# Splitting the loads of double-precision weights, and the GpSimd addition that joins their halves, in an RWKV-7 and quick-GELU kernel

## Chip, cores and metric

One core of a Trainium2 chip runs the kernel. Times are device microseconds of one execution (µs). The time before is the median of three runs, 713.35 µs (712.49 to 715.39).

## What is computed

The reference joins a recurrent attention block and a two-layer block. The recurrence has a 40x40 state for each of 4 batches and 8 heads, over 768 steps; its output, 3072 tokens by 320 channels, goes through two weight matrices with a GELU between them:

```python
for t in range(S):
    y[:, :, t] = np.einsum('bhd,bhde->bhe', rt, state)
    Sa = np.einsum('bhde,bhe->bhd', state, at)
    state = state * wt[:, :, None, :] - np.einsum('bhd,bhe->bhde', Sa, bt) \
            + np.einsum('bhd,bhe->bhde', vt, kt)
x = y.transpose(0, 2, 1, 3).reshape(B * S, H * D)      # 3072 x 320
h = x @ w_in                                           # 320 x 2048
out = (h / (1 + np.exp(-1.702 * h))) @ w_out           # 2048 x 320
```

The activations are float32. The two weight matrices arrive as 8-byte floating-point numbers, because a float32 array times a double scalar is double.

## The kernel before

**Attention.** The sequence is cut into 12 chunks of 64 steps. A chunk and a pair of batches make a *unit*, so there are 24 units. A unit loads its inputs (`load`, L525, and `load_w`, L518), takes logarithms and exponentials of the decay (`decay`, L568), scales its inputs (`prep`, L643), inverts a triangular matrix in five levels (`inverse`, L692: matmuls into `ps_level`, a copy to SBUF at L780 or L813, a transpose at L752 or L731), and solves for its output and the new state (`solve`, L859). The output `x` is written to DRAM and read back transposed as `xT` (`part_with`, L979, and `get_back`, L985), because the two-layer block wants channels on partitions.

**The two-layer block.** For every pair of units, `mlp` (L995) runs the up-projection (`ps_up`), the GELU on ScalarE (L1008) and the down-projection (`ps_down`). All matmuls go through one helper, L330, so the profile tells them apart by the names of their PSUM tiles. The PE instruction stream holds one weight load for each matmul: 20,256 of each.

**The weights.** They stay in SBUF as float32, in `w_sb`. `weight(n, rank, src)` (L462) brings in one of eight *pieces*, each 128 partitions by 1280 numbers of 8 bytes (1280 KB), and turns it into float32 by work on its two 32-bit words. The steps of a piece are:

- L498, SyncE's queue (SP): one transfer from DRAM into a place named by `raws`: a region of `extra`, an unused region of `w_sb`, or two slots of `xT_all`.
- L478, ScalarE: `rebased`, the high word scaled to the float32 exponent.
- L482, L486 and L490, VectorE (DVE): `bounded`, `shifted` and `rounded`, each over 1280 elements.
- L494, GpSimd (POOL): `joined`, an int32 addition of the two parts over 1280 elements, after which the piece counts as `weight`.

Pieces 0 to 3 are `w_in` and 4 to 7 are `w_out`. The first five are loaded in the opening, the others when an earlier piece has left its place.

**What sets the order.** No order is written by hand. Each step is added to a `Plan` (L60) with a rank, the engines that may run it, a cost in ns, what it reads and writes, and for SP steps a size. `Plan.order` (L105) then simulates the engines: whenever an engine is free it takes the runnable step of lowest rank. Its model of the transfers is one wire, used in the order of issue, at 417 bytes per ns with a factor of 1.3, and 2010 ns of latency. It also models the fetch of PE instructions in blocks of 256 (L67): a fetch takes 3528 ns and is stretched while a transfer is under way, with weight 0.35, or 0.63 if the transfer is larger than 1e6 bytes (L68, L204). For POOL and for DVE work in SBUF the model serializes the two engines (L197). `refined` (L247) tries 300 random changes of ranks for steps that start in the first 140 µs and keeps those that shorten the modelled time. So each change of a cost or of a step's size can give another order on every engine in the opening. The emitted program keeps that order for each engine, and waits are put in wherever data or buffers need them.

The ranks of the pieces are `RANKS`, L299: 14, 16, 20, 24, 35, 37, 39, 41. Unit i's loads have rank 10i - 4, its scalings 10i - 6, its solve steps about 10i.

Of the kernel before, what the change touches and what calls it, by code (L numbers as in the profile page):

```python
# [19 lines left out]
INT32 = mybir.dt.int32  # L20
UINT32 = mybir.dt.uint32
INT64 = mybir.dt.int64
ALU = mybir.AluOpType
# [256 lines left out]
def rwkv7_gelu_quick(ctx: ExitStack, tc: tile.TileContext, time_d, v_d, w_d, wc_d, ak_d, b_d, rv_d, w_in, w_out, out):  # L280
    nc = tc.nc
# [5 lines left out]
    PIECE = w_in.shape[2]  # L287
# [6 lines left out]
    EARLY = 4  # L294
    BY_PE = 4
    PLAIN = 4
    ROUNDS, WINDOW, SHARE = 4, 5000.0, 1.0
    TRIES, SEED = 300, 1
    RANKS = [14, 16, 20, 24, 35, 37, 39, 41]  # L299
    HALF = [slice(0, 64), slice(64, 128)]  # L300
    BITS = (0, 1)
# [8 lines left out]
    plan = Plan(dict(logw=3, wc=3, G=1, wch=3, wz=2, time=2, ak=2, b=2, rv=2, FT=3, GT=1, kh=2, bh=2, zr=2, rz=2,  # L310
                     A=1, B=1, RV=2, E0=2, W0=2, P21=2, PT=2, W=2, E=2, ES=2, EX=2, T=2, Tc=1, QT=1, zraw=2, zT=1, M=2, x=1, xT=3, g=4, ob=1), 4)
# [17 lines left out]
    def mm(o, lhsT, rhs, start):  # L329
        nc.tensor.matmul(o, lhsT, rhs, start=start, stop=True, skip_group_check=True)  # L330
# [5 lines left out]
    def pe(*sets):  # L336

        return {"PE": sum(n * 2 * max(58.0, cols / 1.2 + 3) for n, cols in sets), "instr": sum(16 * n for n, _ in sets)}

    def dve(n):  # L340
        return {"DVE": 170.0 + 1.03 * n}

    def act(n):
        return {"ACT": 210.0 + 0.76 * n}
# [7 lines left out]
    def of(e):  # L352
        return nc.gpsimd if e == "POOL" else nc.vector
# [77 lines left out]
    def preset(engine, *places):  # L431
        for t in places:
            copy(engine)(t, one32.unsqueeze(1).to_broadcast([128, 8, 32]))
# [28 lines left out]
    def weight(n, rank, src):  # L462
        at = raws[n]
        def raw():
            if at == "x":
                return xT_all[:, 1:].rearrange("p s n -> p (s n)").bitcast(INT64)
            tile, k = spots[at]
            return tile[:, k * PIECE:(k + 2) * PIECE].bitcast(INT64)

        scale = lambda: w_sb[:, n * PIECE:(n + 1) * PIECE].bitcast(INT32)  # L470

        before = [("weight", m) for m in range(n) if raws[m] == at]
        there = [("weight", m) for m in range(n) if raws[m] in (f"w{n}", f"w{n - 1}")]
        word = lambda dt, w: raw().bitcast(dt).rearrange("p (n two) -> p n two", two=2)[:, :, w]

        def rebased(t):

            nc.scalar.activation(scale().bitcast(FP32), word(FP32, 1), ACT.Prelu, scale=2.0 ** -112, alpha=2.0 ** 32)  # L478

        def bounded(t):  # L480

            nc.vector.tensor_scalar(scale().bitcast(FP32), scale().bitcast(FP32), least, most, ALU.max, ALU.min)  # L482

        def shifted(t):

            nc.vector.tensor_single_scalar(scale(), scale(), 3, op=ALU.logical_shift_left)  # L486

        def rounded(t):

            nc.vector.tensor_single_scalar(word(INT32, 1), word(UINT32, 0), 2.0 ** -29, op=ALU.mult)  # L490

        def joined(t):

            nc.gpsimd.tensor_tensor(out=scale(), in0=scale(), in1=word(INT32, 1), op=ALU.add)  # L494

        one, add = 170.0 + 0.52 * PIECE, 200.0 + 2.1 * PIECE
        T = lambda *names: [(name, n) for name in names]
        plan.add(rank, {"SP": 350.0}, lambda t: nc.sync.dma_start(raw(), src), reads=before, writes=T("wt"), size=128 * PIECE * 8)  # L498
        plan.add(rank, act(PIECE), rebased, reads=T("wt") + there, writes=T("rebased"))
        plan.add(rank, {"DVE": one, "sbuf": True}, bounded, reads=T("rebased"), writes=T("bounded"))  # L500
        plan.add(rank, {"DVE": one, "sbuf": True}, shifted, reads=T("bounded"), writes=T("parts"))
        plan.add(rank, {"DVE": one, "sbuf": True}, rounded, reads=T("rebased"), writes=T("parts"))
        plan.add(rank, {"POOL": add}, joined, reads=T("parts"), writes=T("weight"))

    def weights():
        for n in range(len(raws)):
            weight(n, RANKS[n], w_in[n] if n < NQ else w_out[n - NQ])
# [184 lines left out]
    def inverse(i):  # L692
# [10 lines left out]
        PT = at(PT_t, i).rearrange("p (j t) -> p j t", t=96)  # L703
        if i < PLAIN:
            plan.add(R - 3, {"ACT": 400.0}, lambda t: preset(t.engine, PT[:, :, 64:]), room=T("PT"), writes=T("preset"))
        elif i < PLAIN + 2:
            plan.add(R - 3, {"ACT": 800.0, "DVE": 900.0}, lambda t: preset(t.engine, at(E0_t, i), at(W0_t, i)[:, :, 32:]), room=T("PT"),
                     writes=T("preset"))

        def score_N(t):  # L710

            ps = psum(t, "ps_N")
            for f, u in product(BITS, BITS):
                for e, b in QUARTERS:
                    o, j = (2 * f + u) * 64, slot(b, u, f)
                    mm(ps[HALF[b], e, o:o + 64], ahT()[HALF[e], j], b_of(i)[HALF[e], j], o == 0)
        plan.add(R, pe((4, 64)), score_N, reads=T("ahT", "bhT") + (T("preset") if i < PLAIN + 2 else []), uses=T("ak", "b"), room=T("E0", "P21"), pair=("N", i))
        for n in BITS if i >= PLAIN else ():
            plan.add(R, dve(256), lambda t, n=n: nc.vector.copy_predicated(  # L719
# [4 lines left out]
                 writes=T("P21"), pair=("N", i))  # L724
        if i >= PLAIN:
            plan.add(R, {"DVE": 430.0, "POOL": 750.0, "sbuf": True}, lambda t: of(t.engine).tensor_sub(  # L726
                at(W0_t, i)[:, :, :32], two32.unsqueeze(1).to_broadcast([128, 8, 32]), at(E0_t, i)), reads=T("E0"), writes=T("W0"))

        def turned(rank, source, reads, n, dst, writes):

            plan.add(rank, dve(256), lambda t: nc.vector.transpose(ES(n), source(t)), writes=[key("ES", n, 6)], **reads)  # L731

            def spread(t):
                if t.engine == "ACT":
                    for h in BITS:
                        nc.scalar.activation(dst[:, :, h], ES(n), ACT.Copy, scale=quads[:, h, :1])  # L736
                else:
                    of(t.engine).tensor_mul(dst, ES(n).unsqueeze(2).to_broadcast([128, 8, 2, 32]),
                                            quads.unsqueeze(1).to_broadcast([128, 8, 2, 32]))
            plan.add(rank, {"POOL": 1390.0, "DVE": 700.0, "ACT": 910.0, "sbuf": True}, spread, reads=[key("ES", n, 6)], writes=writes)  # L740

        if i >= PLAIN:
            turned(R, lambda t: at(E0_t, i), dict(reads=T("E0")), 0, EX(0), [key("EX", 0, 5)])
# [411 lines left out]
```

## Time and profile before

| What | Value |
|---|---|
| Median of three runs | 713.35 µs |
| Profiled execution, its own time | 715.64 µs |
| Span of its instructions | 713.9 µs |
| PE busy over the span | 673.0 µs, 94% |
| DVE, ACT and POOL busy | 423.8, 347.7 and 204.6 µs |
| Pieces (L498), transfers | 8, of 1280 KB |
| Issue of such a transfer on SP | 0.33 to 0.41 µs |
| Addition L494, eight times | 2.94 to 3.48 µs |
| L482, L486 and L490, median | 0.82 µs each |
| L478, median | 1.39 µs |

The profile is of one execution, by engine: PE is matmul, PEld is PE's weight load, DVE is VectorE, ACT is ScalarE, POOL is GpSimd, and SPq is the queue of SyncE, which here issues all transfers. A line of a timeline gives the start, the duration, the engine, the line of the code and the instruction with its tiles; a count after x says that a row merges several instructions. In the chain of waits, "issue" is time in which an engine waited for nothing that the records show. The windows give, for a stretch of time, each engine's busy µs and number of instructions, then the clock granted to PE (1.00 is full), the share in which the DMA engines were busy, and GB/s.

### The profile page before, as it was taken

The page shows a single profiled execution, that of the slowest core. Times are in us where ns is not written, and L with a number is a line of the kernel's source. Part 1 is how long each engine was busy: PE and PEld are TensorE (multiplying, and loading weights), DVE is VectorE, ACT ScalarE, POOL GpSimd, SP SyncE. Part 2 cuts the span into 40 slices and gives each one's busy share as a digit, 9 for nine tenths or more (in the row PEclk, how much of TensorE's full clock was granted, in tenths as well). Part 3 has the DMA queues.
Part 4 walks back from the last instruction along what each step waited for, and adds up shares of the span by engine and source line. Part 5 has one row for each costly group of instructions (what it writes and reads, how often), then busy time and mean ns, then how long its engine had stood idle before and what let it go on. Part 6 is the DMA issues. An engine that isn't in the chain of part 4 may idle for free.

```text
span 713.9 us, 43522 instructions
## 1 busy us (share of the span) xinstructions
PE 673.0 (94%) x20256; PEld 562.4 (79%) x20256; DVE 423.8 (59%) x747; ACT 347.7 (49%) x683; POOL 204.6 (29%) x260
## 2 busy tenths in 40 slices
PE   4667899999999999999999999999999999999997
PEld 4566779887888788788888998779978788877563
DVE  6689777756766576577474775666675656421000
ACT  4465636656365465454555565256445535342020
POOL 5367244442431321331342233220341320200000
PEclk9879999999999999999999999999999999999999
DMA  7955351431441341341432241251341230111000
GB/s 244 394 193 181 111 168 47 139 99 44 129 121 32 113 137 32 111 139 42 120 121 86 72 124 50 83 147 33 107 115 32 81 96 5 41 49 31 20 3 19
DMA packets 31860, 69.81 MB, mean 98 GB/s; under 512 B 5056, under 2 KB 14272, under 8 KB 30656
## 3 DMA queue, kind: packets, MB, share of 16 engines
q1 hardware_dynamic: 31680, 67.03, 30.5%
q8 instruction: 159, 2.61, 1.5%
q14 instruction: 21, 0.17, 0.1%
HBM read 59.15 MB, written 7.86 MB: 94 GB/s over the span
## 4 chain that ended last, share of the span: by engine, by line
PE 88%; DVE 5%; issue 3%; DMA 2%; ACT 1%; SPq 0%; ACTq 0%; DVEq 0%
PE ps_down L330 29%; PE ps_up L330 28%; PE ps_level L330 9%; PE ps_y L330 4%; PE ps_B L330 4%; PE ps_X L330 2%; PE ps_T L330 1%; PE ps_Q L330 1%; PE ps_rz L330 1%; PE ps_A L330 1%; PE ps_RV L330 1%; PE ps_N L330 1%; PE ps_zT L330 1%; PE ps_cum L330 1%; DMA rv<-in_rv 1%
## 5 line engine op out<-in xcount | busy, mean ns | idle before, releaser
L330 PE MATMUL ps_up<-xT_all,w_sb 64*64 64x256 f32 x3840 | 251.7, 378 | 1.8 <-issue 1.7
L330 PE MATMUL ps_down<-w_sb,g 64*64 64x320 f32 x3072 | 243.0, 431 | 0.8 <-issue 0.6
L330 PEld LDWEIGHTS ps_up<-xT_all,w_sb 64*64 64x64 f32 x3840 | 157.5, 133 | 27.1 <-issue 2.7
L330 PEld LDWEIGHTS ps_down<-w_sb,g 64*64 64x64 f32 x3072 | 131.1, 133 | 45.4 <-issue 2.4
L736 ACT ACTIVATE EX<-ES,quads 128x256 f32<-128x256 f32 x124 | 56.2, 501 | 56.8 <-DVE ES L731 56.4
L1008 ACT ACTIVATE g<-ps_up 128x1024 f32<-128x1024 f32 x48 | 49.1, 1024 | 39.6 <-PE ps_up L330 39.4
L330 PEld LDWEIGHTS ps_level<-W,EX 64*64 64x64 f32 x2560 | 57.5, 134 | 8.3 <-ACT zT L878 1.0
L780 ACT COPY W<-ps_level 128x512 f32<-128x512 f32 x55 | 32.2, 586 | 55.3 <-PE ps_level L330 54.7
L657 POOL TENSOR_TENSOR kh<-time,G 128x320 f32<-128x320 f32 x23 | 20.9, 910 | 131.9 <-PE ps_y L330 70.7
L330 PE MATMUL ps_level<-W,EX 64*64 64x64 f32 (+1 forms) x2560 | 55.7, 218 | 0.9 <-ACT zT L878 0.6
L782 DVE TENSOR_TENSOR E<-two,ps_level 128x256 f32<-128x256 f32 x80 | 33.2, 415 | 39.1 <-ACT W L780 38.7
L1034 DVE TENSOR_TENSOR ob<-ob,ps_down 128x320 f32<-128x320 f32 x24 | 11.6, 482 | 59.6 <-ACT ob L1032 58.7
L726 POOL TENSOR_TENSOR PT<-two,PT 128x256 f32<-128x256 f32 x18 | 13.1, 728 | 109.8 <-DVE PT L719 105.1
L330 PE MATMUL ps_level<-PT,EX 64*64 64x64 f32 (+2 forms) x1280 | 37.5, 250 | 5.0 <-issue 4.0
L330 PEld LDWEIGHTS ps_level<-PT,EX 64*64 64x64 f32 x1280 | 35.4, 152 | 7.9 <-issue 4.9
L973 POOL TENSOR_TENSOR x<-zr,FT 128x128 f32<-128x128 f32 x80 | 40.9, 539 | 0.0
L731 DVE STREAM_TRANSPOSE ES<-E 128x256 f32<-128x256 f32 x80 | 35.6, 444 | 3.9
L911 ACT COPY B<-ps_B 128x416 f32<-128x416 f32 x38 | 19.1, 504 | 37.2 <-PE ps_B L330 36.9
L330 PE MATMUL ps_y<-RV,kh 64*64 64x104 f32 x768 | 35.7, 251 | 1.4 <-DVE M L927 1.4
L330 PE MATMUL ps_y<-M,bh 64*64 64x104 f32 x768 | 35.6, 249 | 1.2 <-issue 1.2
L649 POOL TENSOR_TENSOR ak<-ak,FT 128x512 f32<-128x512 f32 x16 | 21.5, 1345 | 50.0 <-DMA ak<-in_ak 31.0
L1032 ACT COPY ob<-ps_down 128x320 f32<-128x320 f32 x22 | 9.4, 425 | 53.1 <-PE ps_down L330 53.0
(136 smaller groups left out, 1168.1 us busy)
## 6 DMA issues: line engine op xcount, KB each, us to landing
time<-in_time SPq DMA_DIRECT2D x24, 320.0 KB
ak<-in_ak SPq DMA_DIRECT2D x48, 160.0 KB
rv<-in_rv SPq DMA_DIRECT2D x48, 160.0 KB
xT_all<-x_dram SPq DMA_DIRECT2D x48, 160.0 KB
wc<-in_wc SPq DMA_DIRECT2D x20, 264.0 KB
logw<-in_w SPq DMA_DIRECT2D x24, 160.0 KB
RV<-in_v SPq DMA_DIRECT2D x24, 160.0 KB
b<-in_b SPq DMA_DIRECT2D x48, 80.0 KB
```

What stands on the lines that cost most here:

```text
L330: nc.tensor.matmul(o, lhsT, rhs, start=start, stop=True, skip_group_check=True)
L649: plan.add(R, {"DVE": 690.0, "POOL": 1270.0, "sbuf": True}, lambda t: of(t.engine).tensor_mul(ahT(), ahT(), FT_of(i)), reads=T("ak", "FT") ...
L657: plan.add(R + 4, {"POOL": 870.0, "DVE": 490.0, "sbuf": True}, lambda t, n=n, dst=dst: of(t.engine).tensor_mul(dst(i)[:, :, :D], by_head(t ...
L726: plan.add(R, {"DVE": 430.0, "POOL": 750.0, "sbuf": True}, lambda t: of(t.engine).tensor_sub(at(W0_t, i)[:, :, :32], two32.unsqueeze(1).to ...
L731: plan.add(rank, dve(256), lambda t: nc.vector.transpose(ES(n), source(t)), writes=[key("ES", n, 6)], **reads)
L736: nc.scalar.activation(dst[:, :, h], ES(n), ACT.Copy, scale=quads[:, h, :1])
L780: plan.add(rank, any2(512), lambda t: copy(t.engine)(tiles_of(W(n + 1)), blocks(psum(t, ""), 64)), writes=[key("W", n + 1, 5)], pair=pair)
L782: plan.add(rank, dve(256), lambda t: nc.vector.tensor_sub(tiles_of(E(n + 1)), every(two32, [128, 2, 4, 32]), blocks(psum(t, ""), 64)[:, :, ...
L911: plan.add(R, any2(416), lambda t: copy(t.engine)(dst(), psum(t, "")[:, :, :208]), writes=[("Bv", i)] if x and c > 0 else T("B"), pair=(na ...
L973: of(t.engine).tensor_mul(x[:, b ^ u, b], both(i)[:, at, :64], FT_of(i)[:, at])
L1008: plan.add(-45, {"ACT": 1030.0, "table": "gelu"}, lambda t: nc.scalar.activation(g_of(c * NQ + q).rearrange("p m r n -> p r m n"), psum(t, ...
L1034: plan.add(-45, dve(320), lambda t: nc.vector.tensor_add(ob_of(serial), ob_of(serial), psum(t, "")[:, 1, :DM]), reads=[("ob", serial)], wr ...
```

## The change

Each piece's transfer is issued as four transfers, each of 320 of the 1280 numbers on all 128 partitions (2560 bytes a row in place of 10,240). The ScalarE step waits for all four. The GpSimd addition is issued as two, each over 640 elements; both read the results of the same DVE steps, and a piece counts as done after both. The planner gets four SP steps of 350 ns and a quarter of the size, and two POOL steps of 200 + 1.1 x 1280 = 1608 ns in place of one of 200 + 2.1 x 1280 = 2888 ns. The ranks are unchanged.

```diff
+    PARTS = 4
...
-        def joined(t):
-
-            nc.gpsimd.tensor_tensor(out=scale(), in0=scale(), in1=word(INT32, 1), op=ALU.add)
-
-        one, add = 170.0 + 0.52 * PIECE, 200.0 + 2.1 * PIECE
+        def joined(t, some):
+
+            nc.gpsimd.tensor_tensor(out=scale()[:, some], in0=scale()[:, some], in1=word(INT32, 1)[:, some], op=ALU.add)
+
+        one, add = 170.0 + 0.52 * PIECE, 200.0 + 1.1 * PIECE
...
-        plan.add(rank, {"SP": 350.0}, lambda t: nc.sync.dma_start(raw(), src), reads=before, writes=T("wt"), size=128 * PIECE * 8)
+        for g in range(PARTS):
+            some = slice(g * PIECE // PARTS, (g + 1) * PIECE // PARTS)
+            plan.add(rank, {"SP": 350.0}, lambda t, some=some: nc.sync.dma_start(raw()[:, some], src[:, some]),
+                     reads=before, writes=T("wt"), size=128 * PIECE * 8 // PARTS)
...
-        plan.add(rank, {"POOL": add}, joined, reads=T("parts"), writes=T("weight"))
+        for b in BITS:
+            some = slice(b * PIECE // 2, (b + 1) * PIECE // 2)
+            plan.add(rank, {"POOL": add}, lambda t, some=some: joined(t, some), reads=T("parts"), writes=T("weight"))
```

## The prediction, made before the result was known

> **What bounds the kernel now.** I read the engine totals first, then the stages.
>
> ```profile
> PE 673.0 (94%) x20256; PEld 562.4 (79%) x20256; DVE 423.8 (59%) x747; ACT 347.7 (49%) x683; POOL 204.6 (29%) x260
> ```
>
> ```profile
> 20.00:40.00 20.00, 12.73 (x374) 11.27 (x365) 11.45 (x20) 11.52 (x20) 5.13 (x5) 0.75 0.92 355
> 40.00:60.00 20.00, 15.34 (x592) 14.39 (x595) 18.44 (x22) 12.17 (x31) 14.12 (x12) 0.82 0.49 157
> 60.00:80.00 20.00, 13.87 (x507) 12.34 (x503) 16.40 (x21) 10.52 (x21) 10.77 (x10) 0.91 0.66 210
> 80.00:100.00 20.00, 19.71 (x639) 17.99 (x632) 17.25 (x27) 8.62 (x15) 9.52 (x5) 1.00 0.35 106
> ```
>
> From 80 µs on PE is full. Of some 41 µs without PE work (713.9 - 673.0) about 29 lie before 80 µs, and its clock is also low there (0.75 to 0.91). So only the opening can give time, and µs won there move the full PE stage forward. What holds the opening? The chain of waits (start, duration, what):
>
> ```profile
> 21.58 1.55 issue
> ...
> 27.70 2.10 issue
> ...
> 34.70 1.56 issue
> ...
> 44.06 2.11 issue
> ...
> 52.67 1.35 issue
> ...
> 63.25 2.85 issue
> ...
> 72.35 2.43 issue
> ```
>
> These are two kinds. At 21.58, 27.70, 34.70 and 72.35 PE stops inside a group of matmuls whose inputs are there. The PE timeline counts 127, 128 and 127 matmuls from 23.13 to 29.80, from 29.80 to 36.27 and from 68.26 to 74.78. With the weight loads that is 256 instructions each, in 6.67, 6.47 and 6.52 µs: a block of instructions that arrives late. From 50 to 60 µs, with DMA at 0.26, PE ran 397 matmuls, 3.1 blocks, without such a stop, so a fetch takes at most 3.2 µs there. The slow ones fall where a piece moves.
>
> At 44.06, 52.67 and 63.25 it is DVE that stands, inside an instruction:
>
> ```profile
> 42.12 3.45 POOL L494 TENSOR_TENSOR w_sb<-w_sb 128x1280 int32<-128x1280 int32 x1 [2.00 <-DMA time<-in_time]
> 45.53 1.86 POOL L649 TENSOR_TENSOR ak<-ak,FT 128x512 f32<-128x512 f32 x1
> ```
>
> ```profile
> 42.81 3.45 DVE L486 TENSOR_SCALAR w_sb<-w_sb 128x1280 int32<-128x1280 int32 x1
> 46.18 0.47 DVE L853 SCALAR_TENSOR_TENSOR T<-ps_T,quads,T 128x256 f32<-128x256 f32 x1
> ```
>
> L486 takes 0.79 elsewhere. Here it ends 0.69 after the addition: it waited for the whole of it, then ran, and the next POOL instruction (1.86 in place of 1.27) waited for DVE. So DVE gets its turn between two POOL instructions. L657 at 52.12 (1.97, elsewhere 0.48) and L651 at 63.12 (3.06, elsewhere 0.69) show the same.
>
> Last, SP's queue:
>
> ```profile
> 17.59 3.38 SPq L533 DMA_DIRECT2D b<-in_b  x2
> 24.73 0.35 SPq L533 DMA_DIRECT2D time<-in_time  x1
> 27.82 0.94 SPq L533 DMA_DIRECT2D ak<-in_ak  x2
> 31.84 0.98 SPq L533 DMA_DIRECT2D rv<-in_rv  x2
> 36.41 0.35 SPq L520 DMA_DIRECT2D logw<-in_w  x1
> ```
>
> Counted one by one, each of these waits for the landing of the transfer eight before it, so the five pieces issued from 12.9 to 16.9 landed at about 20.6, 24.7, 27.8, 31.8 and 36.4, at some 415 GB/s.
>
> [...] 159 instruction packets, 2.61 MB, 16.4 KB each. [...] 8 rows of 10,240 B on each of 16 engines at 415/16 = 25.9 GB/s last 3.2 µs, and the late blocks are 3.3 late. [...]
>
> **Part by part.**
>
> *Fetch beside the pieces.* The stops on the chain sum to 1.55 + 2.10 + 1.56 + 2.43 = 7.64. A quarter's share lasts 0.8, so a block should come in 3.2 + 0.8 = 4.0. PE works 4.1 to 4.9 of each such block, so the stops would be gone. At the other end nothing changes, if a fetch is slowed by the traffic and not by one transfer's share. Where they go, the next late thing is the loop from level to level: copy on ACT (0.8), transpose on DVE (0.7), then PE; and at 72.35 the first up-projection needs xT, issued at 74.83. I take 60%: -4.6, between 0 and -7.6.
>
> *The addition in halves.* POOL rows of two inputs take 0.86 for 320 elements and 1.27 for 512, so 640 cost 0.86 + 320 x 2.14 ns = 1.54 and two halves 3.1 against 2.95. L486 came 0.69 into the addition and now waits 0.85 in place of 2.7: 1.85 won. L657 came 1.35 in: some 1.35 won. L651 is followed by the scan L563, [...] which would wait for the second half: 0 won. That is 3.2 on a DVE busy for 18.4 of 20 µs; I take two thirds: -2.1, between 0 and -4.5. The later stalls, as 2.52 for L486 at 85.77, lie beside a full PE: 0; uncovered they would give some 1.3 each. The 8 x 0.15 more of POOL time is hidden by POOL's idle time (29% busy); uncovered it costs 1.2.
>
> *SP.* 24 more issues at 0.35 are 8.4 µs on SP, of which 15 x 0.35 = 5.3 in the first burst. By the eight-back rule the loads of unit 2 behind it (b, time, ak, rv) are issued only when the last eight quarters are left, from about 28 in place of 17.6. They land behind the same bytes as before, by 39.2 (a later issue waits on ak then), and POOL uses ak at 45.53. Cover 6.3 µs: 0. If it were gone, each µs of lateness would cost one. In the planner's order they may even overtake pieces 3 and 4 (ranks 20 and 24 against 16), a gain I don't count. After the piece at 65.65, ak and the x writes (68.56) wait 1.05 longer on SP at most, and the x write waited for POOL there: 0, else 1.
>
> *Smaller rows.* A 10,240 B packet takes 395 ns. Queue 1's other 30,656 packets average 1843 B and, its 30.5% share less the pieces, 100 ns. The line between gives 126 for 2560 B, against 99 for a quarter of a big one: 28% more at worst, 4.5 µs over five pieces; at best 0, [...]. I take 10%, 1.6 µs later. That is inside the 6.3, which the earlier use shrinks to about 2: +0.4, between 0 and +2.5.
>
> *Waits.* L478 waits for four landings in place of one; the last decides, behind it ACT's queue (copies of level results). In the trace it ran well after landing in the first burst (35.03 against 24.7): 0.
>
> *The new order.* All costs feed the planner, so every engine's order in the opening may change. The trace can't price that: 0, between -4 and +4.
>
> Sum: -4.6 - 2.1 + 0.4 = -6.3. The profiled execution took 715.64, 2.3 above the median of 713.35; against the median 707.0.
>
> **Rivals.** *Hidden*: stops turn into waits for ACT, DVE or for unit 2's loads, and at 79 the full stage starts as before, since xT comes behind x, a DRAM write and a piece (the write issued at 68.56, the read at 74.83). For it: DVE is full from 40 to 70, and the longest stop is the last. Against: two stops are DVE's own. Gain 0 to 3, about 712.
>
> *Slower*: the fetch isn't freed, because it is slowed by the total traffic, while the planner, which weighs transfers under 1e6 bytes with 0.35 in place of 0.63, now believes it is and puts more short matmul groups beside the pieces. Each further block caught there costs 6.5 - 3.2 = 3.3; two of them 6.6, so 720. It decides if a block beside quarters still takes over 5 µs. Against it: the 3.2 that a share lasts and the 3.3 of lateness agree.
>
> **How the numbers follow.** A change under 0.5%, 3.6 µs, can't be told from none here. Forecast, 701 to 709.8: 0.52. Hidden, 709.8 to 716.9: 0.26. Slower, above 716.9: 0.22. The range reaches from 700 (the new order's gain added to the forecast) to 719 (most of the slower case).
>
> **What would show it.** Right: 256 PE instructions beside quarters in about 4 µs; additions of 1.5; DVE instructions held no longer than 1.6 by one; PE full before 76. Wrong: blocks still of 6.5; pieces at 320 GB/s; ak of unit 2 landing after POOL is ready for it; or the order of PE so changed that the first up-projection comes after 80.

## The result, and the profile after

The changed kernel took 717.47 µs, the median of 20 runs, against 713.74 for 20 runs of the kernel before beside it: a ratio of 1.0055, with an interval of 1.0036 to 1.0074. It is slower by 0.55%, where 707 was forecast. Every ratio in this document is against runs of the kernel before that were taken beside the others, and leaves out runs more than 1.5% above the fastest of the same kernel: 717.6 and 1151 of e1, and 716.5 of s3. The medians hold all runs, and their quotient can differ from the ratio by up to 0.2%. The profiled execution took 717.18 with a span of 715.4. The changed file's lines have moved: L330, the matmul helper, is now L331, L486 is L487, L494 is L495, L498 is L501 and L651 is L657.

First the engine totals of the kernel after, as on its page:

```profile
PE 669.4 (94%) x20256; PEld 544.8 (76%) x20256; DVE 422.8 (59%) x735; ACT 346.7 (48%) x679; POOL 214.4 (30%) x279
```

PE is without work for 715.4 - 669.4 = 46.0 µs, where before it was 40.9. Next the windows of the kernel after (columns as before: busy time and count of each engine, PE's clock, DMA share, GB/s), and ahead of them one window of the kernel before that the prediction didn't show:

```profile
500.00:600.00 100.00, 99.86 (x3110) 84.54 (x3104) 62.60 (x114) 49.87 (x98) 29.40 (x37) 1.00 0.27 77
```

```profile
20.00:40.00 20.00, 13.96 (x543) 12.44 (x543) 17.29 (x27) 13.88 (x26) 9.55 (x8) 0.91 0.92 299
40.00:60.00 20.00, 12.68 (x510) 11.91 (x510) 12.66 (x20) 10.29 (x19) 6.13 (x9) 0.91 0.74 235
60.00:80.00 20.00, 12.62 (x411) 10.79 (x414) 16.75 (x24) 11.44 (x32) 10.07 (x8) 0.83 0.58 181
80.00:100.00 20.00, 19.96 (x630) 17.48 (x626) 16.05 (x22) 11.08 (x16) 11.53 (x10) 1.00 0.40 123
500.00:600.00 100.00, 96.62 (x3114) 83.18 (x3110) 62.48 (x121) 48.09 (x93) 26.23 (x33) 1.00 0.22 65
```

From 20 to 40 µs PE did 543 matmuls in place of 374: the gain that was forecast, at its place. From 40 to 80 it was given back: 25.3 µs busy in place of 29.2. And a loss that no step of mine looked for stands at 500 to 600, where PE lacks 3.4 µs in a stage that had been full.

The chain of waits of the kernel after, over the opening (start, duration, what), shows where it was given back:

```profile
21.42 0.57 issue
...
25.33 0.75 issue
...
39.68 1.59 issue
...
44.03 3.43 issue
...
51.62 1.39 issue
...
62.51 0.91 issue
63.42 3.08 DVE x L979 x3
...
77.67 2.42 PE ps_up L331 x35
```

The stops that stood at 21.58, 27.70 and 34.70 with 1.55, 2.10 and 1.56 have shrunk to 0.57 and 0.75 up to 30 µs. New ones stand at 39.68, 44.03 (the longest on this chain) and 51.62. SP's queue of the kernel after tells why the first burst is lighter:

```profile
12.40 1.96 SPq L501 DMA_DIRECT2D extra<-in_w_in  x4
14.75 4.63 SPq L501 DMA_DIRECT2D w_sb<-in_w_in  x5
19.94 1.08 SPq L539 DMA_DIRECT2D b<-in_b  x2
21.55 1.10 SPq L539 DMA_DIRECT2D ak<-in_ak  x2
...
27.04 2.37 SPq L501 DMA_DIRECT2D w_sb<-in_w_in  x3
...
29.93 2.06 SPq L501 DMA_DIRECT2D extra<-in_w_in  x4
...
36.76 3.59 SPq L501 DMA_DIRECT2D xT_all<-in_w_out  x4
...
42.97 3.43 SPq L501 DMA_DIRECT2D extra<-in_w_out  x4
```

The planner has made another order. The loads of unit 2 (b, ak) now go in the middle of the third piece that is issued. The fourth, fifth and sixth pieces go at 29.9, 36.8 and 43.0, where before five had been issued by 16.9 and the sixth went at 41.0:

```profile
40.99 0.35 SPq L498 DMA_DIRECT2D extra<-in_w_out  x1
```

POOL starts on unit 2's ak at 28.54 (before: 45.53). So the matmuls run earlier, and the pieces and the additions stand beside other steps than before.

Rows of the timelines of POOL and then of DVE in the kernel after:

```profile
28.54 1.27 POOL L655 TENSOR_TENSOR ak<-ak,FT 128x512 f32<-128x512 f32 x1
29.76 3.55 POOL L495 TENSOR_TENSOR w_sb<-w_sb,extra 128x640 int32<-128x640 int32 x2
...
59.52 3.83 POOL L495 TENSOR_TENSOR w_sb<-w_sb,extra 128x640 int32<-128x640 int32 x2 [6.24 <-DVE w_sb L487]
```

```profile
59.97 2.02 DVE L570 TENSOR_TENSOR_SCAN wc<-starts,wc 128x264 f32<-128x264 f32 x1
61.91 4.59 DVE L979 TENSOR_TENSOR x<-zr,FT 128x128 f32<-128x128 f32 x4
66.42 0.70 DVE L758 STREAM_TRANSPOSE EX<-ps_level 128x512 f32<-128x512 f32 x1
67.06 0.12 DVE L631 TENSOR_TENSOR wz<-wch 128x8 f32<-128x8 f32 x1
```

An addition of two halves stands at 59.52. Beside it the scan takes 2.02 (0.70 elsewhere) and the four x steps 4.59 (0.90 at 649.30). Behind them in DVE's queue stand EX and wz, for which PE waits 3.86:

```profile
67.18 1.56 PE L331 MATMUL ps_level<-PT,EX 64*64 64x96 f32 x32 [3.86 <-DVE wz L631]
...
536.72 0.29 PE L331 MATMUL ps_level<-W,EX 64*64 64x64 f32 x5 [1.58 <-issue]
...
557.74 1.02 PE L331 MATMUL ps_down<-w_sb,g 64*64 64x320 f32 x10 [1.68 <-issue]
```

The last two rows of this timeline of PE are the loss of the late stage: two stops inside groups whose inputs are there, ending 2.58 and 2.44 µs after the start of an instruction packet (534.14 and 555.30); the stops of the opening, on the chain at 21.42, 25.33, 39.68, 44.03 and 51.62, end 2.43 to 2.56 after one. The traces of other kernels have such stops in the full stage too, at other places: 1.74 at 101.4 and 1.15 at 193.6 in the kernel before, 1.45 at 385.1 in e1 below.

### The profile page after: what moved, and what is told of

The parts are those of the page before. It is cut to its first block, busy times and chain, and to the rows that moved or that the text cites. A ratio compares the mean times of both kernels' runs of the same rounds, so it can differ in the third digit from the quotient of the medians.

```text
span 715.4 us, 43589 instructions
## 1 busy us (share of the span) xinstructions
PE 669.4 (94%) x20256; PEld 544.8 (76%) x20256; DVE 422.8 (59%) x735; ACT 346.7 (48%) x679; POOL 214.4 (30%) x279
## 4 chain that ended last, share of the span: by engine, by line
PE 88%; DVE 5%; issue 3%; ACT 2%; DMA 1%; POOL 0%; DVEq 0%; ACTq 0%; SPq 0%
PE ps_up L331 29%; PE ps_down L331 27%; PE ps_level L331 9%; PE ps_y L331 5%; PE ps_B L331 5%; PE ps_X L331 2%; PE ps_Q L331 2%; PE ps_T L331 2%; PE ps_A L331 2%; PE ps_RV L331 1%; PE ps_rz L331 1%; PE ps_N L331 1%; PE ps_zT L331 1%; PE ps_cum L331 1%; DMA b<-in_b 1%
## 5 line engine op out<-in xcount | busy, mean ns | idle before, releaser
L331 PE MATMUL ps_up<-xT_all,w_sb 64*64 64x256 f32 x3840 | 249.8, 378 | 0.3 <-DVE RV L686 0.3
L331 PE MATMUL ps_down<-w_sb,g 64*64 64x320 f32 x3072 | 241.4, 431 | 2.8 <-issue 2.1
L331 PEld LDWEIGHTS ps_up<-xT_all,w_sb 64*64 64x64 f32 x3840 | 153.0, 133 | 30.2 <-issue 0.9
L331 PEld LDWEIGHTS ps_down<-w_sb,g 64*64 64x64 f32 x3072 | 123.5, 133 | 51.5 <-issue 3.4
L331 PEld LDWEIGHTS ps_level<-W,EX 64*64 64x64 f32 x2560 | 56.7, 134 | 12.6 <-ACT EX L742 2.4
L742 ACT ACTIVATE EX<-ES,quads 128x256 f32<-128x256 f32 x106 | 48.1, 501 | 37.3 <-DVE ES L737 37.0
L786 ACT COPY W<-ps_level 128x512 f32<-128x512 f32 x52 | 30.5, 586 | 56.3 <-PE ps_level L331 55.9
L331 PE MATMUL ps_level<-W,EX 64*64 64x64 f32 (+1 forms) x2560 | 55.3, 218 | 1.8 <-issue 1.6
L917 ACT COPY B<-ps_B 128x416 f32<-128x416 f32 x45 | 22.8, 506 | 59.9 <-PE ps_B L331 59.9
L331 PE MATMUL ps_level<-PT,EX 64*64 64x64 f32 (+2 forms) x1280 | 33.2, 238 | 8.6 <-DVE wz L631 3.9
L331 PEld LDWEIGHTS ps_level<-PT,EX 64*64 64x64 f32 x1280 | 31.2, 141 | 11.8 <-DVE wz L631 4.0
L933 DVE TENSOR_TENSOR M<-ps_X,later 128x832 f32<-128x832 f32 x24 | 24.5, 1022 | 21.3 <-PE ps_X L331 21.3
L331 PE MATMUL ps_y<-RV,kh 64*64 64x104 f32 x768 | 35.8, 250 | 1.3 <-DVE M L933 1.2
L331 PE MATMUL ps_y<-M,bh 64*64 64x104 f32 x768 | 35.7, 249 | 0.0
L660 POOL TENSOR_TENSOR ak<-ak,GT 128x512 f32<-128x512 f32 x20 | 31.5, 1573 | 10.4 <-DMA ak<-in_ak 10.4
```

Source lines behind the costliest of these rows:

```text
L660: plan.add(R, {"DVE": 690.0, "POOL": 1270.0, "sbuf": True}, lambda t: of(t.engine).tensor_mul(khT(), khT(), GT_of(i)), reads=T("ak", "GT") ...
L786: plan.add(rank, any2(512), lambda t: copy(t.engine)(tiles_of(W(n + 1)), blocks(psum(t, ""), 64)), writes=[key("W", n + 1, 5)], pair=pair)
L917: plan.add(R, any2(416), lambda t: copy(t.engine)(dst(), psum(t, "")[:, :, :208]), writes=[("Bv", i)] if x and c > 0 else T("B"), pair=(na ...
L933: plan.add(R + 1, dve(832), lambda t: nc.vector.tensor_tensor(M_of(i).rearrange("p (j b) n -> p b j n", b=2), psum(t, "")[:, :, :416].rear ...
```

## The experiments

Two theories. *Order*: the two splits by themselves cost nothing, and the loss comes from the other order that the planner made of the changed costs. *Instructions*: the splits themselves cost time (24 more issues, smaller rows, more blocks caught beside the pieces), in whatever order.

### The splits in the old order

The planner is given the old step with its old cost; only what the step emits is changed. In e3 the transfer alone, in e4 the addition alone, in e1 both.

```diff
-lambda t: nc.sync.dma_start(raw(), src)
+lambda t: [nc.sync.dma_start(raw()[:, q * PIECE // 4:(q + 1) * PIECE // 4], src[:, q * PIECE // 4:(q + 1) * PIECE // 4]) for q in range(4)]
...
-            nc.gpsimd.tensor_tensor(out=scale(), in0=scale(), in1=word(INT32, 1), op=ALU.add)
+            for h in BITS:
+                some = slice(h * PIECE // 2, (h + 1) * PIECE // 2)
+                nc.gpsimd.tensor_tensor(out=scale()[:, some], in0=scale()[:, some], in1=word(INT32, 1)[:, some], op=ALU.add)
```

> The whole change in its instructions (four transfers, two additions), but planned as before: every engine keeps the order of the kernel before. If the loss of 3.7 us comes from the instructions themselves (smaller rows, 24 more issues and landings on SP, SP held by the rule of eight), this kernel is slower than before by 3 to 4 us. If it comes from the order that the planner made anew, this kernel is not slower: as in the prediction's sum of -6.3 at best, and at least within 1.5 us of before.

> Only the four transfers, in the old order. If the fetch of PE instructions is freed and that counts (the prediction's largest term), 2 to 5 us faster than before, with blocks of 256 PE instructions in 4.0 to 4.8 us between 20 and 37 us, where before has 6.5. If the next late thing takes it all, blocks as short but the time within 1.5 us. If quarters cost as such, 2 us or more slower.

> Only the two additions, in the old order. By the prediction's term 1 to 2 us faster, with L486 at 43 us held for 0.9 in place of 2.7. By the rival, that DVE and PE's other waits cover it, within 1 us of before. If DVE is only held twice in place of once, no gain and up to 1 us slower.

Beside 713.24 for the kernel before: e1 711.29 (0.9959, interval 0.9940 to 0.9979), e3 713.05 (1.0007, 0.9984 to 1.0031), e4 711.78 (0.9979, 0.9962 to 0.9996). So the same instructions that made the kernel slower make it faster in the old order.

The quarters alone make no difference that can be told from none. PE's timeline and SP's queue of e3:

```profile
24.29 0.49 PE L330 MATMUL ps_level<-PT,ident 64*64 64x128 f32 x3 [1.67 <-issue]
...
31.38 0.63 PE L330 MATMUL ps_cumc<-edges,logw 64*64 64x65 f32 x28 [2.82 <-issue]
```

```profile
16.05 6.13 SPq L498 DMA_DIRECT2D w_sb<-in_w_in  x8
...
31.26 1.13 SPq L533 DMA_DIRECT2D b<-in_b  x2
...
33.65 1.12 SPq L533 DMA_DIRECT2D ak<-in_ak  x2
```

The block between the two stops took 31.38 - 24.29 = 7.1 µs beside quarters, longer than any beside whole pieces (6.7). That is none of the three outcomes expected for e3: the blocks stayed slow and the time stayed the same. The loads of unit 2 went out at 31.3 in place of 17.6, and the time shows no cost of it.

The halves do what was worked out, and one thing more. DVE's timeline of e4:

```profile
42.41 2.07 DVE L486 TENSOR_SCALAR w_sb<-w_sb 128x1280 int32<-128x1280 int32 x1
...
45.43 1.04 DVE L653 SCALAR_TENSOR_TENSOR b<-b,GT 128x512 f32<-128x512 f32 x1
...
50.81 0.72 DVE L659 TENSOR_TENSOR kh<-time,G 128x320 f32<-128x320 f32 x1
...
52.05 1.26 DVE L659 TENSOR_TENSOR bh<-time,G 128x320 f32<-128x320 f32 x1
...
61.51 1.67 DVE L653 SCALAR_TENSOR_TENSOR b<-b,GT 128x512 f32<-128x512 f32 x1
63.10 2.08 DVE L565 TENSOR_TENSOR_SCAN wc<-starts,wc 128x264 f32<-128x264 f32 x1
```

Before, these took 3.45, 0.74, 1.97, 0.56, 3.06 and 0.96 (L659 was L657, L653 was L651, L565 was L563). L486, kh and the later b win 1.38, 1.25 and 1.39. But each time a step further on in DVE's queue now stands beside the second half and loses: the first b 0.30, bh 0.70, the scan 1.12. Together DVE gets 1.9 of 4.0 µs.

### The new order by itself, and each split in it

Here the planner gets the changed steps and makes the changed order, but only the first quarter's step issues a transfer, of the whole piece, or only the first half's step issues an addition, of the whole. e2 has both, n1 only the whole addition (so quarters), n2 only the whole transfer (so halves).

```diff
-lambda t, some=some: nc.sync.dma_start(raw()[:, some], src[:, some]),
+lambda t, g=g: nc.sync.dma_start(raw(), src) if g == 0 else None,
...
-lambda t, some=some: joined(t, some), reads
+lambda t, some=some, b=b: joined(t, some) if b == 0 else None, reads
```

> The other half: the order of the changed kernel on every engine, with whole transfers (issued in the place of the first quarter) and whole additions (in the place of the first half). If the order is the cause, it is slower than before by 3.7 us or more, since the fetch is slow beside whole pieces again. If the instructions are the cause, it is within 1.5 us of before.

> The order of the changed kernel with its four transfers, but each addition whole, in the place of its first half. The changed kernel is 8.7 us faster than the same order with whole transfers and whole additions. If the transfers bring that (in this order SP puts unit 2's loads between the quarters of the pieces, which a whole piece can't), this kernel is within 3 us of the changed kernel, some 716 to 720. If the halves bring it, it is at 722 or more.

> The order of the changed kernel with its two additions, but whole transfers, each in the place of its first quarter. If the halves bring the 8.7 us, within 3 us of the changed kernel; if the transfers do, 722 or more. In the old order the halves alone were worth 1.5 us, the quarters nothing.

e2 took 726.16 (1.0176, 1.0134 to 1.0218; 6 runs), n1 718.46 (1.0097, 1.0058 to 1.0135; 4 runs beside 711.43), n2 720.43 (1.0123, 1.0078 to 1.0168; 4 runs). The changed kernel has both splits: 1.0055. In the new order the two splits together bring 1.0176 - 1.0055 = 1.2%, with 0.5% of uncertainty (the intervals combined as root of squares). The quarters by themselves bring 0.8%, with 0.6% of uncertainty; the halves 0.5%, also with 0.6%, so theirs can't be told from none. By the ratios n1 is 0.4% and n2 0.7% above the changed kernel: neither split alone brings the whole. So the splits help in this order too, and it is the order that costs. One limit: in that order one quarter of the third piece stands ahead of unit 2's loads, and in e2 and n2 the whole of it moves there, so they are the order with a heavier first burst.

The wait for wz, 3.86 in the kernel after, is 4.14 in n1, 4.32 in e2 and 4.20 in n2, and in no trace of the old order. In n1, where the addition is whole, the scan takes 3.40 and the four x steps 3.21 (timeline at 59.96 and 63.28): 6.61 together, just as 2.02 + 4.59 with the halves. So this hold belongs to the order, and halving the addition only moved it from one step to the next.

The windows of e2, to be held against those of the kernel after:

```profile
40.00:60.00 20.00, 14.98 (x427) 14.10 (x424) 10.16 (x16) 8.18 (x16) 8.36 (x7) 0.59 0.72 230
60.00:80.00 20.00, 13.31 (x443) 12.19 (x435) 14.65 (x19) 9.07 (x21) 6.63 (x4) 0.78 0.35 118
```

and one of e1:

```profile
60.00:80.00 20.00, 15.95 (x577) 14.32 (x573) 17.20 (x25) 11.35 (x26) 9.08 (x10) 0.91 0.67 209
```

With the same instructions as the kernel after, PE was busy for 15.95 of these 20 µs in e1, and for 12.62 in the kernel after.

To see where one execution leads another, I weight each matmul of the trace with the mean spacing of its kind in the trace of before, sum up to a time, and subtract. The profiled executions of e1 (711.26) and after (717.18) both lie at their medians, so they can be compared, though each is a single execution:

| Lead in PE work, µs | at 40 | at 80 | at 120 | at 500 | at 600 | at 690 |
|---|---|---|---|---|---|---|
| after, over before | +4.1 | +1.3 | +1.4 | +3.9 | -0.7 | -1.4 |
| e1, over before | +0.3 | +3.3 | +5.1 | +5.0 | +4.8 | +4.2 |
| after, over e1 | +3.8 | -2.0 | -3.7 | -1.1 | -5.5 | -5.6 |

Against e1, the changed kernel loses 7.5 between 40 and 120, wins back 2.6, and loses 4.4 between 500 and 600. What PE waited for in the opening, in µs by what ended the wait ("issue" is a stop inside a group, where the profile shows no wait):

| PE idle, µs | 12 to 40: issue | other engines and loads | 40 to 120: issue | DVE | ACT, POOL |
|---|---|---|---|---|---|
| before | 5.2 | 2.0 | 5.4 | 6.2 | 2.3 |
| e1 | 6.2 | 3.2 | 4.4 | 2.8 | 0.5 |
| after | 2.8 | 5.6 | 7.5 | 7.1 | 1.2 |

From 12 to 120 µs the stops inside groups sum to 10.3 in the kernel after and 10.6 in e1: the new order moved them to a later place and did not add to them. What grew are the waits for other engines, above all for DVE between 40 and 120 (7.1 in place of 2.8; 3.86 of it is the wait for wz).

The stops of 1.58 and 1.68 in the late stretch are in the rows of PE above. n1 has them too, at the same two places (1.6 and 1.4), e2 the first of them (1.6), n2 and e1 neither. All stops over 0.5 µs of this kind from 90 µs on sum to 4.3 in after, 2.9 in before, 2.1 in e1 and 2.3 in n2, which has the order of after. So it is not shown that the late stage's loss belongs to the order.

### How far orders differ by themselves

The planner's random search was started from another number (`TRIES, SEED = 300, 1` to 2 or 3), in the kernel before (s1, s2) and in the changed one (s3, s4).

> The kernel before, with only the seed of the planner's 300 random trials changed (2 in place of 1), so the instructions are the same in another order. If the new order made by the change is one draw among orders that the planner takes for about equal, this one differs from before by some 2 to 10 us, more likely slower. If the planner's orders are alike in time, it is within 1.5 us of before, and the 12.6 us of the order alone need a cause in the change itself.

> As the run with seed 2, with seed 3: by the draw theory 2 to 10 us off before and not the same amount as seed 2; by the other within 1.5 us.

> The changed kernel with seed 2. By the draw theory it differs from the changed kernel by some 2 to 10 us, to either side, and stands on average no worse than the kernel before with the same seeds. If the change's plan (transfers of a smaller size, which the planner takes to slow the fetch less) is worse in itself, it is as slow as the changed kernel or slower, and slower than before's order with the same seed by 3 us or more.

> The changed kernel with seed 3. By the draw theory 2 to 10 us off the changed kernel, to either side; if the change's plan is worse in itself, as slow as the changed kernel or slower, and 3 us or more above the kernel before with seed 3.

Beside 711.62: s1 709.65 (0.9976, 0.9959 to 0.9992), s2 714.35 (1.0045, 1.0022 to 1.0067), s3 711.96 (1.0000, 0.9974 to 1.0026), s4 714.14 (1.0045, 1.0026 to 1.0065). Without any change to an instruction the order moves the time over 0.7%. s1 came out faster, which had been thought the less likely side, and s4 is neither 2 µs off the changed kernel nor 3 above s2. The changed kernel ranges over 0 to 0.55%, with the order of the change at the upper end, beside s4.

Then the best of these orders with the splits emitted inside single steps, as in e4 and e1:

> A version that may beat both: the order that the kernel before gets with seed 2 (1.7 us faster than before), with the additions in halves. If halves are worth in any order what they were in the old one, 1 to 2 us less than that, some 708; if their gain hangs on the order, within 1 us of the run with seed 2.

> As the last one, with the four transfers too. In the old order both together were 2.9 us faster than before, with the halves alone at 1.5: if the transfers add something by themselves, 1 us or more below the kernel with halves alone; if not, within 1 us of it. PE's blocks of 256 instructions beside the pieces should again take 5 us or more.

Beside 711.43: b1 709.03 (0.9977, 0.9955 to 0.9999), b2 707.66 (0.9954, 0.9930 to 0.9977). b2 is the fastest version found, but its interval and that of e1 (0.9959) can't be told apart. The halves alone added nothing to s1 (0.9977 beside 0.9976, where 1 to 2 µs had been expected), so their gain hangs on the order; the quarters on top of them brought 0.2%, inside the noise.

b2 and s3 have the same splits and the same start of the search. They differ only in what the planner was told: s3 planned with the changed costs and sizes, b2 with the old ones. s3 is slower by 0.46%, with 0.35% of uncertainty, as the changed kernel is slower than e1 by 0.96%. So at both starts where both were run, the plan made for the split steps was the worse one. That speaks for a fault in what the planner believes of split steps, beside the luck of a draw; two starts don't prove it. A plan of the split steps in which quarters keep the weight of whole transfers (0.63) would tell, and wasn't run.

### What slows the fetch

e3 left open why a block comes late beside pieces. In f1 and f2 the kernel before issues quarters, but each only once the quarter two (f1) or four (f2) before it has landed; an 8-byte read of that quarter, issued ahead, makes SP wait: the first 20 quarters went out from 12.69 to 48.63 in f1, and from 13.23 to 36.75 in f2.

```diff
+            if len(sent) >= 2:
+                nc.sync.dma_start(probe, sent[-2])
             nc.sync.dma_start(raw()[:, some], src[:, some])
+            sent.append(raw()[:1, some.start:some.start + 1])
```

> The old order with four transfers a piece, and before each quarter an 8-byte read of the quarter two before it, so that SP issues a quarter only when that one has landed: at most two under way. Whole pieces and quarters up to eight deep gave PE blocks of 256 instructions every 5.2 to 7.1 us beside the pieces. If the fetch is slowed by what is queued or moved in all, blocks now come in 4.5 us or less, while the pieces run at some 200 to 250 GB/s and SP is held for longer. If it is slowed by any transfer of this kind under way, still 6 us.

> The same with four quarters under way. Four of 320 KB should keep the rate near 400 GB/s with half the bytes queued. If the depth of the queue is what slows the fetch, blocks lie between those with two and with eight, some 5 us. If the rate moved is, they are as with eight, 5.8 us or more.

f1 took 735.05 (1.0287, 1.0206 to 1.0368; 2 runs), f2 715.24 (1.0023, 1.0000 to 1.0047). The windows of f1, then of f2, then of e3:

```profile
20.00:26.00 6.00, 4.89 (x209) 4.31 (x208) 4.63 (x8) 3.57 (x6) 0.54 (x1) 1.00 0.72 205
26.00:32.00 6.00, 3.72 (x159) 2.99 (x148) 4.80 (x7) 4.30 (x11) 3.81 (x2) 1.00 0.70 200
```

```profile
20.00:26.00 6.00, 4.08 (x161) 3.56 (x161) 5.69 (x9) 3.15 (x4) 1.46 (x2) 1.00 0.90 281
26.00:32.00 6.00, 4.23 (x116) 3.99 (x120) 2.50 (x4) 2.66 (x10) 2.08 (x2) 0.72 0.95 310
```

```profile
20.00:26.00 6.00, 3.30 (x119) 2.92 (x114) 3.56 (x6) 2.37 (x4) 1.45 (x2) 0.81 1.03 389
26.00:32.00 6.00, 3.18 (x122) 2.94 (x120) 4.69 (x7) 1.60 (x2) 0.00 (x0) 0.90 1.04 393
```

The starts of PE's instruction packets (16,384 bytes each) in the traces give the time between two fetches in this stretch: 4.0 to 4.3 µs with two quarters in flight at about 200 GB/s, 4.4 to 6.2 with four at about 300, 5.2 to 7.1 with up to eight at 390 (e3), 6.1 to 6.8 with whole pieces at 418. In f1 this holds up to 26 µs; the next packet comes after 5.6, with PE waiting for DVE and no stop inside a group. Where no piece moves, from 50 to 62 in the kernel before, they are 3.7 to 4.3 apart. The packet itself takes 1.0 to 1.2 µs in the first burst of the kernel before and 0.9 to 1.7 over the whole run: what comes late is its start. So in these runs the fetches stood further apart the more was in flight and moved, and smaller single transfers didn't free them. Which of the two, queue or rate, isn't separated: with four in flight both fell. The rate alone doesn't explain it: in the kernel after, the packets between 19 and 27 µs stand 3.8 to 4.2 apart, with 302 GB/s moved from 20 to 26, and those between 39 and 50 µs 5.5 to 6.2 apart, with 307 GB/s from 37 to 50. f1 as a whole is slower, with late pieces and SP held; which of these costs isn't separated.

## Why the prediction was wrong

The sum by its own terms, in µs of some 713:

| Term | Forecast | Measured | What shows it |
|---|---|---|---|
| Fetch beside the pieces | -4.6 | about 0, with the third row | e3: +0.5, interval -1.1 to +2.2 |
| Addition in halves | -2.1 | -1.5 | e4: -2.7 to -0.3 |
| SP, smaller rows, waits | +0.4 | in the first row | e3 holds these too |
| New order | 0 | +6.8 | after against e1: 1.0055/0.9959 |
| Sum | -6.3 | +3.9 | e1: -2.9, then +6.8 |

The first three rows measured one by one give -1.0, and both splits at once (e1) -2.9; the 1.9 between them lies within the intervals. In the prediction itself, the lower end of its range is not the sum that it names: 707.0 - 4 is 703, and not 700.

**The new order** is the step that turned the sign. I wrote that the trace can't price it and took 0, between -4 and +4. It cost 6.8, or 4.9 to 8.8 with the intervals of both ratios combined as root of squares: more than the bound that I gave it. The bound had no measurement behind it. That the order is the cause is shown, since e1 has the same splits. Where it costs is shown in part. PE's waits for other engines grew in the opening, above all the 3.86 behind the addition at 59.5, which stands ahead of x and wz on DVE. The stops inside groups have moved from the first burst to the pieces at 36.8 and 43.0 (1.59, 3.43 and 1.39), with the same sum as in e1. That these waits make up the 6.8 is argued only, since none was taken away alone, and the two late stops may be chance.

**The fetch** failed as a mechanism. I took the time that one transfer's share lasts, 3.2 µs, for the lateness of a block, because both numbers agreed. In the traces each record of a piece is one row, 0.39 µs (10,240 B), and 0.10 as a quarter (2560 B). That a fetch waits for a whole share of 8 rows was assumed, and no record shows it. With quarters a block took 5.2 to 7.1 in e3, and not 4.0, so the length of one transfer's share is not what makes it late. The agreement was also less close than it looked: the 3.2 for an undisturbed fetch came from a count of matmuls between 50 and 60 µs, where the instruction packets start 3.7 to 4.3 apart, so the late blocks of the first burst (6.1 to 6.8) are some 2 to 3 late. In the changed kernel packets start 3.8 to 4.8 apart up to 27 µs, and 5.2 to 6.2 apart from there to 50. The short ones fit the lighter first burst that the order makes; f1 shows the same with less in flight.

**The halves** held in the mechanism and in part in the size: L486 was to win 1.85 and won 1.38, L657 1.35 and won 1.25, and the scan took most of L651's gain. That the second half would hold other steps behind L486 and L657 too was not counted. It took back 0.30 and 0.70, so DVE won 1.9 in place of 3.2, and that the share of two thirds (2.1) lies near the measured 1.5 is luck in part. In e4 the scan at 63.10 took 2.08 beside the second half of the addition, 0.96 before: held for 1.12, as was expected of it. What I left out is that another order can put other DVE work beside the additions. The x steps at 61.91 (4.59 in place of 0.90) are such work, and with them PE stood for 3.86.

**Smaller rows**: 28% at worst, 10% taken. In the first burst the median packet of 2560 B takes 104 ns in e3, so four take 416 against 388 for one of 10,240 B in the kernel before: 7%. The rate fell by as much, from about 418 GB/s to about 391. **SP**: unit 2's loads were issued late as worked out (from about 28 forecast, 31.3 in e3), and the cover held.

**The rivals.** The slower one named the outcome, and its condition holds in the old order: a block beside quarters takes over 5 µs. But in the old order that costs nothing, since nothing is put beside it that wasn't there. Its mechanism, the planner trusting shorter transfers and putting matmul groups beside them, fits the stops at 39.68, 44.03 and 51.62, and b2 against s3 speaks for it. But the stops in the opening sum to no more than in e1, so the further blocks that it counted on are not the loss; DVE's hold at 59.5 and the late stage are outside it. *Hidden* is seen up to 40 µs: against before, the stops fell from 5.2 to 2.8, and the waits for other engines and loads rose from 2.0 to 5.6. The first up-projection started at 77.53 in place of 79.23, so the opening was shortened by 1.7 and not by 6.

Two things stay open. Why the fetches behind 536 and 557 came late: from 530 to 534 the DMA engines moved nothing, so the first isn't traffic; before the second they moved 172 GB/s (552 to 555). And what the quarters win in the new order (0.8%): it may be a freer fetch or the early loads of unit 2.

## What to carry to other kernels

Where a planner sets the order, an edit to one instruction is two changes: measure the edit with the order held (let one planned step emit the new instructions), and the new order with other starts of the search, before either is believed. Before you split a GpSimd instruction that holds a DVE instruction, look at what the second half will hold: here it took back half of what DVE won (2.1 of 4.0 µs in e4). Splitting a transfer freed nothing for instruction fetch here (blocks 5.2 to 7.1 µs apart in e3, 6.1 to 6.8 before); fewer transfers in flight did (4.0 to 4.3 in f1, up to 26 µs), at the price of later data (the twentieth quarter issued at 48.63).

## What the runs showed of the hardware

In after PE stopped for 1.58 µs, up to 536.72, where the DMA engines had moved nothing from 530 to 534. n1 and e2 stop by 1.6 at the same matmul, n2, which shares their order, doesn't. The packets of 2560 B took 7% more than those of 10,240 B for the same bytes in the first burst (4 x 104 ns in e3, 388 ns before), and the kernel showed no difference in time (e3: 1.0007, interval 0.9984 to 1.0031). Two additions of 640 took 3.08 µs undisturbed (at 50.20 in after; one of 1280 took 2.95 at 32.30 before), and up to 4.25 beside DVE work (at 82.15 in after, with DVE's L483 up to 82.75 and its L487 from 84.15 to 84.96 beside them).
